# Cross network on one core: the last jobs in another order, with group 6's output transposes and store in other places of the queues

## The chip, the core and the metric

The kernel runs on one core of a Trainium2 chip. Matrix products run on TensorE (PE), evacuations of PSUM with the bias on ScalarE (ACT), products and sums in bf16 on VectorE (DVE); SyncE (SP) issues nearly all DMAs, GpSimd (POOL) has a few copies. The metric is the device time of one execution in microseconds (us).

## The reference

```python
B, F, D, L = 16384, 26, 16, 6          # Din = F * D = 416
x = x0                                 # (16384, 416) bf16
for l in range(L):                     # ws (6, 416, 416), bs (6, 416)
    x = x0 * (einsum('bd,de->be', x, ws[l]) + bs[l]) + x
return x
```

## The kernel before

**Groups, jobs, tiles.** The 16384 rows are cut into 8 groups of 2048 (g = 0 to 7). A job (g, l) is layer l of group g. The features lie on the partitions: 416 = 3 x 128 + 32. The three blocks of 128 output features are the job's three tiles (i = 0, 1, 2), each of four chunks of 512 rows (j); the last 32 features are the job's tail, and the tails of two or three jobs are computed together, in a "tail phase" (`tails`, L677). A chunk takes 13 slots of TensorE time in quarters: 12 for the three blocks of 128 input features and one for the 32. A tile's chunk goes PSUM -> ACT (adds the bias, writes `tw`) -> DVE (times x0, in pairs of chunks) -> DVE (plus x, writes the next layer's `x`).

**Order.** The list `order` (L322 to L328) says in which order the 48 jobs run; a job of layer l needs all tiles and the tail of layer l-1 of its group. `batches` cuts that list into tail phases. `items` (L943) is the list of tiles and phases. From tile 1 of job (0, 2) to tile 0 of job (7, 4) the items run as one stream (`stream`, L1005): each chunk is done as row-tiled matmuls of 32 input rows, and the string `ORDER` (L204) says, letter by letter, which chunk is given the next free row group; "|" is a tail phase. `replay` (L230) turns the string into a list with a place in time for each matmul (20 units are one matmul of 512 columns) and for each evacuation. What stands behind the stream runs as whole 128-row matmuls (`full`, L629) and 32-row ones (`rows32`, L657). In the last stream tile only the 32-row part is in the stream; its 12 full matmuls follow it.

**The end.** Job (7, 5) is not tiled like that: its output comes in natural layout (L1116 to L1232), in four rounds kk of four products, each of 128 rows x 416. A product goes through ACT (`nat_out`, L1180), then DVE multiplies it by x0 (`nat_mul`, L1185) and adds x (`nat_add`, L1191), and SP stores the round (`nat_store`, L1199). The x to be added must be in natural layout too: `rest_turn(t)` (L922) transposes tile t of x(7, 5) (which is what job (7, 4) wrote) by DMA into `x5n`, for t = 0 and 1; tile 2 and the tail are transposed by TensorE (`turn_last`, `turn_tails`) and copied by DVE (L1150) and ACT (L1163). `nat_add` of round 0 waits for all of these.

**Output of the other groups.** `output(g)` (L876) is called when the last tile and the tail of (g, 5) are both done. It issues on SP a DMA transpose for each tile (`turn(t)`, into the one buffer `ost`), one of the tail (into `ot3`), and the store; `spread` copies `ot3` into `ost`, on POOL for groups 0 to 5, on ACT for group 6. `ost` is one buffer, so group g+1's transposes wait for group g's store to land. `prefill` (L615) issues DMAs that rotate a tail by 32-partition steps, for a later job of the same group; `tails` calls it for each job of the phase, followed by `done_with`, which may call `output`. SP runs its queue in order: whatever waits there holds all that follows.

**The last items before the change**, in order: (5, 5), (7, 3) tile 0, a phase [(5, 5), (7, 3), (6, 4)], the rest of (7, 3), (6, 4), and (7, 4) tile 0, where the stream ends; then (6, 5) tiles 0 and 1, a phase [(7, 4), (6, 5)], (6, 5) tile 2, (7, 4) tiles 1 and 2, and job (7, 5).

Of the kernel before, what the change touches and what calls it, by code (L numbers as in the profile page):

```python
# [21 lines left out]
class Program:  # L22
# [176 lines left out]

SLOT = 20  # L200
FENCE, PHASE, CHANGE = 22, 52, 9
READ, NEXT, BACK, SECOND, PAIR, TAILS, SUMS = 19, 56, 70, 92, 56, 220, 240
LETTERS = "ABCDEFGHIJKLMNOPQRSTUVWXYZabcdefghijklmnopqrstuvwxyz0123456789"
ORDER = (  # L204
    "ABCDAJCXaFTMWDUNSLYBKTMZjGANDaMpCPUJCXIROEDBaTUJCITVCQLVCAXNaALVaQHNKUTBQKDRICbRK|AJDWQJDCfUNSDM"
    "dSbJECbURCTINWDUJSPAJCTAZSPUJCDVYOTJAaDYVKTENCbNUSDJAXSYJGPAVODNUDOJUTCIRCDUNSbAJTaMVKHQBCXQNCPI"
    "ZSDJQCDMVaTEJOXBUDOAZXOIRGDYBSXARLOYBXKMZG|QBPSIVDCPAZOXQJGDQBaTINCLAdSXJYOHRACTNUCPJUSDAVCXRMaL"
    "FUCXARWPYBKPAdaLUNCLMVTCNISDcBWPIRCLAVSbMBKPYVSHMB|CTMVCPIVCDUNaTIBaTVAKTNUGDMVSDINCXYJCDMVSbIFW"
    "PQBCTMVCPIVSDIBWTANKTYVODAZOTUJGDURODINCbUJODBMSbIVCTUBSPIVGDQVCTMJWDAZSXINGDUBSXIBKTAZKPcRGAZPW"
    "QBP|QBOLRECTBCUPZSAPRaXASJPUBKUDVSAPRKAbSNcDOUbFKDURKDIRCbQJOXBIODVAOTUJCLQVCDUNSbEJWDQVCTINCbUJ"  # L210
    "ODIBaTVAKTNUGDMVSDINCXBcXSNAKPAZWLAVKTYNGDYNSDYN|ICXJTACVQPCNAPeVAPeRYLWNQDKNbCIBWTYBSLMVCLMVCXM"
    "JSDAdWPQBLOQBbKNQCDdMWTZEODNUKTABOXAVCTcVOLERCDcRaPAJWbMRKHYBCXQNCPIZSDJQCDMVaDMJSbAJTOYVGDMVCjU"
    "N|ISDJTAKRMDJCQDNeITVGMbBWIDRWIDRKAbJSMDBObQJCDdOQXJaMDJWMTBKAXhSMDJOUDVKQPFCMDBaQfVKALRWMDJOUDV"
    "KATBOYjREWDROULBKUTBSIBLCUdCMLZSAbJSUDRKMXeFLQBCXMR|CPISFDQCTIBaDUZKDQJWbMBXOIZCLQBSbIdODIVCTUJO"
    "DIVODIBbCNYXKERDCUdTaIBTaJUOHAVCTMVKDUJSDAVCXQNKDYJWfAJWTMZGDMVCXcNS|IDJTECRCTANaDYVKTMFWDUBOXAN"
    "KXZQODZATOJUCLURODINCbIBWTJYOHAVCTMVKDUJSDIRDCUNSbBISbVAKPURCLMRWDINCXIBWTJgOHAVCTMVKDUJSDAVCXQN"
    "KDYJSfAJaPURGDMdCbUN|ISDJTECRCTANaDMVKTFYWDAVOTYJGXAVODNUDOJUTCIRODIBSbUJPCIVDQCZTMBaLMBaXIBWLQZ"
    "ODIZCXQZKPAJWDRMWDNUKTBISBDUORbAOZDaULNQGXJCQXBAWPRaIDRKUDJSUPGBAbVCMDVOYLFSUPBeMXRCM|RCPISFDQCT"
    "IBaTIVOHQBPCMVDOAZWPBUOLQBCfURODIdWPQZGDQNCbINWDINXGQBPAWBQPKVDIVSPAJODYJCXQKZPEBWDQNWLAVKTAJSAD"
    "OVYDNKTYBKbMVSHBeMXRCM|RCPISFDQCDMVaTIBSbUBTKMVCLMVSDIBSXIZDKURDSMJCbIBSXIZOHQBCTMVCPIVSDQJCTIBa"  # L220
    "DUZSLAJbQOVHAOBbUOBLUChTIVOALVOQDJCXQBiLMSVDKMBbWJMHCVASXdIDJSUPCJUDSVIDSBMbRCMLRCcbJOALVMaDJMaD"
    "JYOXRAO|ANXKQBLSABOXYRGLMVDWNACbNQWDNISDJAWfBcSXJMGbVQCPRCPISFDAeTUBKTMVCLUNSDMJTCIBWTIdOHQBPCMV"
    "DOAZWPBUKDQVCfIRWPYFCXQZCPIRWDJQWPEBCTAZSPUJCLAZCXMRaLUBWLAVLSgNXGIRCDUNS|IDJTAKRMDJCQbJWATVCQPJ"
    "WALBaUTBODUadTIGVATVOIDJWAXRKYPFCMDBaMTCZMLRWALRCAfROUDJeUTaBQPKVEDVSMDJOAfJCQXKZMDJWATJWMDVKMTB"
    "CARaXMBKPZUDWRIPaAJbCYVTO|EJDWQBPCNAbOVLQCJDUiRLaAJbSUNDKMXCBMTWJYHOAVPCMVDOUBPWIRDIORXENKLAUKBN"
    "CD"
)


def replay(tails, events, needs, keep, part):  # L230

# [14 lines left out]
    home, read, out, latest, due = {}, {}, [], [[]] * 4, list(events)  # L246

    def over(now):
        nonlocal act
# [8 lines left out]
    for letter in ORDER:  # L258
        if letter == "|":
            now, m = min(free), due.pop(0)  # L260
            parts = [(f - now) // SLOT for f in free]
            at = now + max((f - now) % SLOT for f in free)
            over(at)
            on = at + 3 * SLOT * m + PHASE
            moved = [on + SLOT * k for k in parts]
            for f in flight.values():
                f[1] = moved[f[2]] if f[1] == free[f[2]] else -9 * SLOT
            got = [banks.pop(0) for _ in range(m)]
            assert all(t <= at + 3 * SLOT * k for k, (t, _) in enumerate(got))
            for r in range(4):  # L270
                for k in range(parts[r]):
                    latest[r][-1 - k][0] = moved[r] - SLOT * (k + 1)
            for k, (_, b) in enumerate(got):
                if k == 1:
                    banks.append((on + SECOND, b))
                    continue
                start = max(act, on - CHANGE + READ)
# [28 lines left out]
def bass_standalone__cross_network_dcn__recsys_kernel(  # L306
# [7 lines left out]
    L = ws.shape[0]  # L314
# [223 lines left out]
    def evacuate_chunk(g, l, i, j, b, read):  # L538
# [33 lines left out]

        todo = [multiply, plus]
        if len(out_) == NJ:
            todo.append(lambda: finish_tile(g, l))
# [101 lines left out]
    def tails(batch, corners_last=False, banks=None):  # L677
# [38 lines left out]
        while later:  # L716
            load_group(later.pop(0))
# [158 lines left out]
    def output(g):  # L876

        s, s3 = xset[(g, L)], xtail[(g, L)]
        def turn(t, j0=0, j1=NJ):
            add("sp", lambda h: h.dma_start_transpose(  # L880
                ost[:, j0 * KK:j1 * KK, t * P:(t + 1) * P], xs[s][:, t * GC + j0 * CH:t * GC + j1 * CH]),
                reads=[("x", s, t, j) for j in range(j0, j1)], writes=[("ost", t, j) for j in range(j0, j1)],
                lane="ot" if g < LAST - 1 else f"ot_{t}{j0}", batch=g)

        turn(0)
        if g == LAST - 1:
            turn(1)
        add("sp", lambda h: h.dma_start_transpose(ot3[:, :, :], x3s[s3][:, :]),
            reads=[("x3", s3)], writes=["ot3"], lane="ot3", batch=g)
        if g < LAST - 1:  # L890
            spread("pool")
            turn(1)
            turn(2)
            store(g, 0, NJ)
        else:
            turn(2, 0, 2)
            turn(2, 2, NJ)
        free_x.append(s)
        free_3.append(s3)

# [30 lines left out]
                writes=[("x5n", j, t) for j in range(j0, j1)], lane=f"x5_{t}{j0}", batch=0)  # L931

    items = []
    where = {(b[0 if b in batches[4:-3] else min(1, len(b) - 1)], 0): b for b in batches[:-1]}
    where[((LAST - 1, L - 1), 1)] = batches[-1]
    behind = ("tile", (LAST, L - 2), 0)
    del where[((0, 0), 0)]
    where[((0, 1), 0)] = where.pop(((1, 0), 0))
# [4 lines left out]
        if (jb, i) in where:  # L943
            items.append(("tails", where[(jb, i)]))

    for i in range(1, NT):
        late = items.index(("tile", (LAST, L - 2), i))
        items.append(items.pop(late))


    single = 0
    k = 0
    while k < len(items):
        if items[k][0] == "tails":
            if single % 2 == 0:
                nxt = k + 1
# [3 lines left out]
                    k += 1  # L960
            single = 0
        else:
            single = 1 if items[k] == behind else single + 1
        k += 1

    W_LOAD = {(1, 0): 3, (0, 2): 4, (1, 1): 5}
# [12 lines left out]

    tiles_done = {}  # L980

    def finish_tile(g, l, n=1):
# [22 lines left out]
    def stream(run, keep, part):  # L1005
# [9 lines left out]
        place = {it: NJ * k for k, it in enumerate(tiles)}  # L1015
        needs = [[(t, place[(g, l - 1), t]) for t in range(NT if c < len(chunks) - keep else part)
                  if c - place.get(((g, l - 1), t), -99) < 30] for c, ((g, l), i, j) in enumerate(chunks)]
        plan, read, left = replay([quad(g, l, j)[0] for (g, l), i, j in chunks], [len(b) for n, b in due],
                                  needs, keep, part)
# [58 lines left out]
    for n, it in enumerate(items):  # L1078
# [200 lines left out]
```

## Time and profile before

| | |
|---|---|
| runs, median of 3 | 467.83 us (467.56 to 467.90) |
| profiled execution | 467.5 us, its span 465.7 us |
| PE, DVE, ACT busy | 99%, 87%, 81% of the span |
| granted TensorE clock | 0.997 |
| DMA | 53.77 MB, mean 115 GB/s |

The profile gives busy times of each engine, the groups of instructions by source line, the chain of waits that ended last, and a timeline. In a timeline row the first number is the start in us from the span's beginning, the second how long the row's instructions took together, "SPq" an instruction of SP's queue (a DMA being issued, not its transfer), and a note in brackets the idle time before it and who ended it.

### The profile page before, as it was taken

How to read it: one execution, taken by the hardware profiler on the slowest of the kernel's cores; microseconds unless marked ns; L12 is line 12 of the kernel's file. 1: busy time of each engine (PE TensorE's matmuls, PEld its weight loads, DVE VectorE, ACT ScalarE, POOL GpSimd, SP SyncE). 2: the span in 40 equal slices, each digit the busy share in tenths (PEclk: the TensorE clock that was granted, in tenths of full speed). 3: DMA queues.
4: the chain of work that ended last, by engine and by line, in shares of the span. 5: the costliest groups of instructions: out<-in, count | busy, mean ns of one | idle time of the engine just before them, and what ended most of it. 6: DMA issues, size and time to landing. Idle time of an engine off the chain costs nothing.

```text
span 465.7 us, 17469 instructions
## 1 busy us (share of the span) xinstructions
PE 458.9 (99%) x7827; PEld 263.8 (57%) x7833; DVE 404.2 (87%) x700; ACT 379.1 (81%) x608; POOL 6.8 (1%) x15
## 2 busy tenths in 40 slices
PE   9999999999999999999999999999999999999995
PEld 5444566555556677555655556565575566755442
DVE  2887998989989899979989898888989889898897
ACT  4687888788888888888878888788887887889785
POOL 1000000000000000000000000000000000000000
PEclk9999999999999999999999999999999999999998
DMA  8986949101002978084858437990100095027899
GB/s 229 185 177 144 160 113 190 29 3 26 1 4 38 158 210 155 22 141 149 149 92 154 145 78 141 160 296 23 25 2 4 25 148 172 14 49 169 183 161 292
DMA packets 139087, 53.77 MB, mean 115 GB/s; under 512 B 112762, under 2 KB 138500, under 8 KB 139012
## 3 DMA queue, kind: packets, MB, share of 16 engines
q1 hardware_dynamic: 138856, 52.54, 52.5%
q8 instruction: 61, 1.00, 0.9%
q10 hardware_dynamic: 156, 0.11, 0.1%
q14 instruction: 14, 0.11, 0.1%
HBM read 5.97 MB, written 13.63 MB: 42 GB/s over the span
## 4 chain that ended last, share of the span: by engine, by line
PE 93%; DVE 4%; DMA 1%; issue 1%; ACT 0%; SPq 0%; DVEq 0%
PE ps L1040 70%; PE ps L697 7%; PE ps L1044 6%; PE ps L650 6%; PE ps L638 2%; PE ps L685 1%; DMA wm<-in_ws_dram 1%; DVE x L1194 1%; DVE x L1188 1%; DVE x L528 1%; DVE tw L523 1%; PE ps L671 1%; ACT tw L514 0%; PE ps L789 0%; SPq L734 0%
## 5 line engine op out<-in xcount | busy, mean ns | idle before, releaser
L1040 PE MATMUL ps<-x,wm 32*128 32x512 bf16 x6000 | 356.0, 374 | 0.0
L550 ACT ACTIVATE tw<-ps,bias 128x512 bf16<-128x512 f32 x500 | 310.5, 688 | 46.4 <-PE ps L1040 35.9
L1040 PEld LDWEIGHTS ps<-x,wm 32*128 32x128 bf16 x6000 | 212.5, 92 | 127.7 <-ACT tw L550 4.1
L562 DVE TENSOR_TENSOR tw<-tw,x 128x1024 bf16<-128x1024 bf16 x250 | 168.2, 689 | 39.6 <-ACT tw L550 38.9
L567 DVE TENSOR_TENSOR x<-tw,x 128x1024 bf16<-128x1024 bf16 x250 | 163.5, 690 | 0.3
L1044 PE MATMUL ps<-x,w 32*128 32x512 bf16 x504 | 151.7, 374 | 0.0
L1044 PEld LDWEIGHTS ps<-x,w 32*128 32x128 bf16 x504 | 42.7, 92 | 6.6
L514 ACT ACTIVATE tw<-ps,bias 128x512 bf16<-128x512 f32 (+1 forms) x46 | 35.0, 839 | 12.0 <-PE ps L671 7.9
L650 PE MATMUL ps<-x,wm 128*128 128x512 bf16 x146 | 33.6, 379 | 1.0 <-issue 0.8
L697 PE MATMUL ps<-x,wm 128*32 128x512 bf16 x564 | 33.6, 380 | 0.0
L608 ACT ACTIVATE ts<-ps,bias 128x512 bf16<-128x512 f32 x33 | 21.0, 687 | 14.7 <-PE ps L685 14.7
L523 DVE TENSOR_TENSOR tw<-tw,x 128x1024 bf16<-128x1024 bf16 (+1 forms) x35 | 21.4, 627 | 4.9 <-ACT tw L514 4.7
L650 PEld LDWEIGHTS ps<-x,wm 128*128 128x128 bf16 x152 | 13.9, 98 | 19.0 <-issue 3.2
L697 PEld LDWEIGHTS ps<-x,wm 128*32 128x32 bf16 x564 | 13.5, 96 | 18.7 <-ACT tw L550 4.7
L528 DVE TENSOR_TENSOR x<-tw,x 128x1024 bf16<-128x1024 bf16 (+1 forms) x35 | 20.6, 624 | 0.0
L612 DVE TENSOR_TENSOR x<-ts,x 128x512 bf16<-128x512 bf16 x47 | 18.4, 420 | 0.4
L610 DVE TENSOR_TENSOR ts<-ts,x 128x512 bf16<-128x512 bf16 x33 | 13.0, 418 | 0.0
L604 DVE SCALAR_TENSOR_TENSOR ts<-ps,bias,x 128x512 bf16<-128x512 f32 x14 | 10.5, 748 | 2.2 <-PE ps L685 2.2
L909 POOL COPY ost<-ot 128x512 bf16<-128x512 bf16 x6 | 5.3, 890 | 411.3 <-DMA ot<-x 411.3
L1130 PE MATMUL ps<-wm,x 128*128 128x416 bf16 x48 | 9.8, 340 | 0.1
L1182 ACT ACTIVATE x<-ps 128x416 bf16<-128x416 f32 x16 | 7.6, 518 | 2.4 <-PE ps L1130 2.4
L799 DVE COPY x<-ps 128x512 bf16<-128x512 bf16 x5 | 2.0, 423 | 8.5 <-PE ps L789 8.5
(50 smaller groups left out, 76.9 us busy)
## 6 DMA issues: line engine op xcount, KB each, us to landing
out_dram<-ost SPq DMA_DIRECT2D x6, 1664.0 KB, 7.1
x<-x SPq DMA_DIRECT2D x24, 96.0 KB, 2.3
x<-in_x_dram SPq DMA_DIRECT2D x8, 208.0 KB, 4.4
x<-in_x_dram SPq DMA_DIRECT2D x4, 416.0 KB, 8.0
out_dram<-ost SPq DMA_DIRECT2D x2, 832.0 KB, 6.0
wm<-in_ws_dram SPq DMA_DIRECT2D x5, 312.0 KB, 3.4
x<-x SPq DMA_DIRECT2D x22, 64.0 KB, 2.0
out_dram<-x SPq DMA_DIRECT2D x3, 416.0 KB, 4.8
```

The costliest lines, as they stand in the source:

```text
L514: add("act", lambda h, a=a, w=w, b0=b0: h.activation(tw[r][:, a * CH:(a + w) * CH], psum[:, b0 * CH:(b0 + w) * CH], ACT_F.Identity, bias=b ...
L523: add("dve", lambda h, a=a, e=e: h.tensor_tensor(tw[r][:, a * CH:e * CH], tw[r][:, a * CH:e * CH], x0s[s0][:, i * GC + a * CH:i * GC + e * ...
L528: add("dve", lambda h, a=a, e=e: h.tensor_tensor(xs[so][:, i * GC + a * CH:i * GC + e * CH], tw[r][:, a * CH:e * CH], src(i, a, e), ALU.ad ...
L550: add("act", lambda h: h.activation(tw[r][:, j * CH:(j + 1) * CH], bank(b), ACT_F.Identity, bias=bias[:, i, l:l + 1], scale=1.0), reads=[( ...
L562: add("dve", lambda h: h.tensor_tensor(tw[r][:, o], tw[r][:, o], x0s[s0][:, c], ALU.mult), reads=[("tw", r, k) for k in both] + [x0_tok(s0 ...
L567: add("dve", lambda h: h.tensor_tensor(xs[so][:, c], tw[r][:, o], src(i, a, a + 2), ALU.add), reads=[("tw", r, k) for k in both] + [stok(i ...
L608: add("act", lambda h: h.activation(ts[r][:, :], bank(b), ACT_F.Identity, bias=bias[:, 3, l:l + 1], scale=1.0), reads=[("ps", b), "bias"], ...
L612: add("dve", lambda h: h.tensor_tensor(x3s[so][:, :], ts[r][:, :], res, ALU.add), reads=[("ts", r)] + rtok, writes=[("x3", so), ("x3", so, ...
L650: add("pe", lambda h, t=t, j=j, k=k, w=w: h.matmul(bank(banks[j])[:, k * w:(k + 1) * w], wm[l][:, t, ecols], src(t, j, j + 1)[:, k * w:(k ...
L697: add("pe", lambda h, t=t, j=j, src=src, l=l, b=b, ro=ro, qo=qo: h.matmul(psum[qo, b * CH:(b + 1) * CH], wm[l][:, t, NT * P:D], src(t, j, ...
L1040: add("pe", lambda h, l=l, t=t, j=j, b=b, q=q, ecols=ecols, src=src, kw=kw: h.matmul(bank(b), wm[l][q, t, ecols], src(t, j, j + 1)[q, :], ...
L1044: add("pe", lambda h, l=l, b=b, q=q, ecols=ecols, s3=s3, kw=kw: h.matmul(bank(b), w3[l][q, ecols], s3[q, :], **kw), reads=tok3 + [("w3", l ...
```

## The change

`order`'s last jobs become (6, 3), (5, 5), (7, 2), (6, 4), (7, 3), (6, 5), (7, 4), (7, 5). The last three phases are written out: [(5, 4), (6, 3), (7, 2)], [(5, 5), (6, 4), (7, 3)], [(6, 5), (7, 4)]. The two late tiles of (7, 4) are no longer moved behind (6, 5) by hand. So the stream, which ends at (7, 4) tile 0 as before, now holds the three tiles of (6, 5) and the phase [(6, 5), (7, 4)] as well; behind it only (7, 4) tiles 1 and 2 are left. Within the stream a phase is no longer put behind the tile that follows it when the count of tiles is odd, so most phases stand one tile sooner; `ORDER` is a new string, and `replay` has a new condition: a chunk of (g, l) starts no sooner than 600 units after the phase of (g, l-1) ended (`ROTATE`).

In the queues: the tile transposes of groups 5 and 6 are issued by `finish_tile` as each tile ends, those of groups 0 to 4 by `output` as before. In `tails`, all jobs' `prefill` rotations are issued ahead of `done_with`, and group 6's tail transpose right behind its phase. Group 6's `spread` (ACT) and its two stores (SP) are issued behind the last tile of (7, 4).

The sequence on SP from the phase of (5, 5) on is, before: group 5's tail transpose, its tiles 1 and 2, its store, four rotations, `rest_turn(0)`, group 6's tiles 0 and 1, its tail, its tile 2 in two halves, `rest_turn(1)` in two halves, group 6's two stores, and the stores of group 7. After: four rotations, group 5's tail transpose, its store, group 6's tile 0, its tail, its tile 1, its tile 2 in two halves, `rest_turn(0)`, `rest_turn(1)` in two halves, and the stores.

```diff
-    order[-6:] = [(5, 5), (7, 3), (6, 4), (7, 4), (6, 5), (7, 5)]
+    order[-8:] = [(6, 3), (5, 5), (7, 2), (6, 4), (7, 3), (6, 5), (7, 4), (7, 5)]
...
+    batches[-3:] = [[(5, 4), (6, 3), (7, 2)], [(5, 5), (6, 4), (7, 3)], [(6, 5), (7, 4)]]
...
+            if after[c] is not None:
+                start = max(start, past[after[c]] + ROTATE)
...
+        for g, l in batch if corners_last else ():
+            prefill(g, l + 1)
+            filled.add((g, l + 1))
+        if (LAST - 1, L - 1) in batch:
+            turn_tail(LAST - 1)
         for g, l in batch:
-            if corners_last:
-                prefill(g, l + 1)
-                filled.add((g, l + 1))
             done_with(g, l)
...
+    def output(g):
+
+        s, s3 = xset[(g, L)], xtail[(g, L)]
+        if g < LAST - 2:
+            turn(g, 0)
         if g < LAST - 1:
+            turn_tail(g)
             spread("pool")
-            turn(1)
-            turn(2)
+            if g < LAST - 2:
+                turn(g, 1)
+                turn(g, 2)
             store(g, 0, NJ)
-        else:
-            turn(2, 0, 2)
-            turn(2, 2, NJ)
...
-    for i in range(1, NT):
-        late = items.index(("tile", (LAST, L - 2), i))
-        items.append(items.pop(late))
...
-    while k < len(items):
+    while items[k] != ("tile", (0, 2), 1):
...
+    def finish_tile(g, l, n=1, i=None):
+        if l == L - 1 and g > LAST - 3:
+            turn(g, i)
...
         if (g, l) == (LAST, L - 2) and i < NT - 1:
-            if i:
-                spread("act")
             rest_turn(i)
+        elif (g, l) == (LAST, L - 2):
+            spread("act")
+            store(LAST - 1, 0, 2)
+            store(LAST - 1, 2, NJ)
...
-    store(LAST - 1, 0, 2)
-    store(LAST - 1, 2, NJ)
```

More of the change, by code (lines that the diff above doesn't have):

```diff
@@ L201 @@
 FENCE, PHASE, CHANGE = 22, 52, 9
-READ, NEXT, BACK, SECOND, PAIR, TAILS, SUMS = 19, 56, 70, 92, 56, 220, 240
+READ, NEXT, BACK, SECOND, PAIR, TAILS, SUMS, ROTATE = 19, 56, 70, 92, 56, 220, 240, 600
 LETTERS = "ABCDEFGHIJKLMNOPQRSTUVWXYZabcdefghijklmnopqrstuvwxyz0123456789"
 ORDER = (
[L205 to L226, printed above, removed]
@@ new lines @@
+    "ABCDAJCXaFTMWDUNSLYBKTMZjGANDaMpCPUJCXIROEDBaTUJCITVCQLVCAXNaALVaQHNKUTBQKDRICbRK|AJDWQJDKbQBSDQ"
+    "dKbMFCbMVSDMJCXIZSDJAXSIBKTYBSLUZDKMVTCMJSDIZOTEBPCUBPSAZLCRUKDdQaXJAWTYJGPAVODNUDOJUTCIBCbUNKDI"
+    "daTMVCPJUaTFA|RODMLFCAXYSBPQCZPIWRALROUDKBQXaJATKVASLVMCLBYSXNICDZMWDVMSDNICfVISbBSbJUOHAVCTMVKD"
+    "UJSDIRPCANbCVMSLYBLORUHBeMXRCM|RCPISFDAWTIBKDUZKDgRKbMVCXJMaTFAODVATOJUCLURODARCfYRWLARXOANLYBaL"
+    "QVCLcNSXEKRDAWNDUOJTAKRATCNDUaNLcGBTMWZHSBMbCVM|RCPISFDQCDMVaTIBSbUBTKMVCLMVSDANSXAdTOJUDJCYTVAO"
@@ new lines @@
+    "BPcWJDUeRbIGVPCUBTMWBPIWRDICTVCMJDWcRLaMXFCMTBaIDVSIPFCUPRCADRaUPFKQDaNQXCIBXSIZHOQBPCMVLCAZDaRM"
+    "DaNIXCVcTOJYXSFA|RODMLFCAXYSBPQCZPIWRALROUDKBQXaJATKVASLVMGDBYSXJATCZMSLVEODNUCDRAafJQPGBbMCZULS"
+    "BIeTZODIVCTUJODIVODIBbCNYXCIVSPAdaLUBWLMRHKBYXRCM|RCPISFDQCDMVaTEJOXBUPCAZPSUBPKQVDKQBTaAZKDQZKX"
+    "MFSDYBXOAdKXQNCLMZSDINTCANWDVgSLENXKBUTCAVPYCVLMSBDMeVLSYFXCMVTCMJDWIZPSFAPCUBPSIVHCURPCMBaDMZLC"
+    "IVTaMFDOYVDMJWfAVK|MBXKNALWNQCDNQCbJAWTBQePJCfQZWPERCPAWJPgSHARCTYNKDUJSDIRPCANbSBYSLVATKUNCLMVS"
@@ L227, with replay @@
+    "UPCJAbSVIDSJUDRKUPBKAbRWMDJCYTVOIHBAaXBQOLVcGDVQODJMeXRAK|MBXKNALWNQCDNAWbJAWTBSPcJUGbNQKHVEOLBC"
+    "DANCXMKBLYCVTYeNHAaVfQGJ|ADCRUbCJTAgSJbMiVLQWBTMVCD"
 )
-def replay(tails, events, needs, keep, part):
+def replay(tails, events, needs, after, keep, part):
     n = len(tails)
@@ L245, in replay @@
     banks = [(0, 0), (0, 1), (0, 2), (0, 3), (84, 4), (84, 5), (178, 6), (178, 7)]
-    home, read, out, latest, due = {}, {}, [], [[]] * 4, list(events)
+    home, read, out, latest, due, past = {}, {}, [], [[]] * 4, list(events), []
     def over(now):
@@ L874, in load_last, with turn @@
                 reads=["brow"], writes=[("brow", j)], lane="brow", batch=0)
[L876 to L880, printed above, removed]
+    def turn(g, t):
+        s = xset[(g, L)]
+        halves = ((0, 2), (2, NJ)) if (g, t) == (LAST - 1, NT - 1) else ((0, NJ),)
+        for j0, j1 in halves:
+            add("sp", lambda h, j0=j0, j1=j1: h.dma_start_transpose(
                 ost[:, j0 * KK:j1 * KK, t * P:(t + 1) * P], xs[s][:, t * GC + j0 * CH:t * GC + j1 * CH]),
@@ L933, in bass_standalone__cross_network_dcn__recsys_kernel @@
     items = []
-    where = {(b[0 if b in batches[4:-3] else min(1, len(b) - 1)], 0): b for b in batches[:-1]}
-    where[((LAST - 1, L - 1), 1)] = batches[-1]
+    where = {(b[0 if b in batches[4:-3] else min(1, len(b) - 1)], 0): b for b in batches[:-3]}
+    where.update({((5, 4), 1): batches[-3], ((6, 4), 1): batches[-2], ((6, 5), 1): batches[-1]})
     behind = ("tile", (LAST, L - 2), 0)
@@ L962, in bass_standalone__cross_network_dcn__recsys_kernel @@
         else:
-            single = 1 if items[k] == behind else single + 1
+            single += 1
         k += 1
@@ L1017, in stream @@
                   if c - place.get(((g, l - 1), t), -99) < 30] for c, ((g, l), i, j) in enumerate(chunks)]
+        phase = {jb: k for k, (n, b) in enumerate(due) for jb in b}
         plan, read, left = replay([quad(g, l, j)[0] for (g, l), i, j in chunks], [len(b) for n, b in due],
-                                  needs, keep, part)
+                                  needs, [phase.get((g, l - 1)) for (g, l), i, j in chunks], keep, part)
         at = list(ring)
```

19 lines of the change are left out of this document (14 added, 5 removed).

## The prediction, as it stood before the run

> **What bounds the kernel now.** First the page: where the time is, and the chain that ended last.
>
> ```profile
> span 465.7 us, 17469 instructions
> PE 458.9 (99%) x7827; PEld 263.8 (57%) x7833; DVE 404.2 (87%) x700; ACT 379.1 (81%) x608; POOL 6.8 (1%) x15
> PE 93%; DVE 4%; DMA 1%; issue 1%; ACT 0%; SPq 0%; DVEq 0%
> ```
>
> TensorE carries 93% of the chain; the stream has no gap to win. The rest is DVE, and the chain in order of time shows where: PE to 442.8 us, then without a break DVE to 462.4. So the end is asked for next: the timeline of DVE and ACT.
>
> ```profile
> 446.88 1.36 DVE L523 TENSOR_TENSOR tw<-tw,x 128x1024 bf16<-128x1024 bf16 x2
> 452.04 1.38 DVE L1150 COPY x<-ps 128x1024 bf16<-128x1024 bf16 x2
> 453.34 1.14 DVE L1188 TENSOR_TENSOR x<-x,x 128x832 bf16<-128x832 bf16 x2
> 454.39 1.08 DVE L1194 TENSOR_TENSOR x<-x,x 128x832 bf16<-128x832 bf16 x2
> ...
> 442.76 4.75 ACT L514 ACTIVATE tw<-ps,bias 128x1024 bf16<-128x1024 f32 x7 [0.98 <-PE ps L671]
> 447.54 0.63 ACT L907 ACTIVATE ost<-ot 128x512 bf16<-128x512 bf16 x1
> 448.07 2.41 ACT L514 ACTIVATE tw<-ps,bias 128x512 bf16<-128x512 f32 x4
> ```
>
> No DVE row has a bracket: from 446.88 on it has no wait worth naming. L1194 at 454.39 is the first `nat_add`, which needs `rest_turn`'s transposes. ACT is late for the last tile because of a backlog and the `spread` copy (L907). Third, SP's timeline, for what each queued DMA waits behind:
>
> ```profile
> 427.55 0.41 SPq L916 DMA_DIRECT2D out_dram<-ost  x1
> 428.00 1.96 SPq L444 DMA_DIRECT2D x<-x  x1
> ...
> 435.23 1.81 SPq L928 DMA_TRANSPOSE x<-x  x1
> 438.85 5.67 SPq L880 DMA_TRANSPOSE ost<-x  x2
> 444.57 1.69 SPq L888 DMA_TRANSPOSE ot<-x  x1
> 446.39 2.62 SPq L880 DMA_TRANSPOSE ost<-x  x2
> 449.05 2.72 SPq L928 DMA_TRANSPOSE x<-x  x2
> 451.95 1.87 SPq L916 DMA_DIRECT2D out_dram<-ost  x2
> ```
>
> SP issues from 442.6 to 453.2 with hardly a pause; `rest_turn(1)` (L928, two halves at 449.05 and 450.4) stands behind all of group 6. Last, the load of the DMA engines by stretches (columns from the end: GB/s, DMA share, clock):
>
> ```profile
> 442.58:452.00 9.42, 9.21 (x67) 4.26 (x61) 8.94 (x20) 8.29 (x14) 0.00 (x0) 1.00 0.88 170
> 456.00:464.00 8.00, 4.73 (x32) 2.15 (x30) 6.25 (x14) 4.14 (x8) 0.00 (x0) 0.95 1.11 333
> ```
>
> The engines are nearly full on both sides: on transposes at 170 GB/s, then on stores at 333. After 446.88 the end is set by DVE, with the DMA queue close behind.
>
> **The stream and TensorE.** Work is only moved. The stream gains three tiles and a phase of two tails. Two phases starting at 238.26 and 266.08 lie 2574 of `replay`'s units apart: 27.82 us, so one slot of 20 units is 0.216 us. Three tiles are 3 x 13 x 0.216 = 8.4 us; the phase is 24 of the 36 column matmuls that take 2.06 us, 1.4, with corners and the change of shape 1.9; the new string leaves 0.1 us less empty: 10.2 us later. The twelve full matmuls of (7, 4) tile 0, loaded from 429.44, move to 439.6. Behind them stand two tiles: 2.70 (429.44 to 432.14) + 0.33 (32-row part, 445.57 to 445.90) + 2.70 + 0.33 + 2.60 (445.90 to 448.50) = 8.66, so job (7, 5) starts at 448.26 instead of 448.50: **-0.24**. The phases that stand one tile sooner, and ROTATE, cost the order no slot; group 4's load falls behind a rotation that waits for the phase at 79.8, near 86 instead of 68.7, and is used at 176.
>
> **ACT and DVE at the end.** The stream's last evacuation starts near 441.3 (its place in the order), then four of about 0.6 for tile 0, to 444.3; tile 1's banks are full at 444.8 to 445.4, so ACT is through it at 447.25 and through tile 2 at 449.6 (before: 450.48), since `spread` now stands behind. DVE is the slower one: from 438.9 on it has (6, 5) tiles 1 and 2, (7, 4) tiles 0 and 1, 16 operations of 0.61 (1.29 for two, overlapped) = 9.8, one wait for ACT of 0.3, then eight of 0.335 (2.7), to 451.7 instead of 452.12. The copies and the products of (7, 5) also wait for TensorE, which gains 0.24, so no more than that is counted: the first `nat_add` could start at 454.2 instead of 454.39, its second half at 454.7 instead of 454.90: **-0.2**. Moving `spread` earns nothing more, as DVE covers it; ACT has a pause of 0.9 ahead of `nat_out`, where it fits.
>
> **SP.** Group 6's first transpose needs its tile on DVE and group 5's store landed. The phase of (5, 5) moves to 419.5; rotations at 423.3 and, behind five more DVE operations, 425.2 (0.6 us per DMA), group 5's tail transpose 426.4, landing 2.95 later, POOL copy 0.93, store 430.5, landing 6.8 later (the row of 427.55), 437.3. DVE reaches (6, 5) tile 0 only at 438.2, because its second pair stands behind the tail of (7, 4). So the series starts at 438.2, 0.6 sooner than the 438.85 of before, but `rest_turn(0)` (435.23 before) is now inside it: tile 0 of (7, 4) ends at 446.4 instead of 435.2. The work in the series grows from four tile transposes and a tail to five and a tail. Issue by rows: first 2.0 (1.8 to 2.9), tail 1.7 (1.3 to 2.1), tile 1 2.3 (1.9 to 2.9), tile 2 in halves 2.7, `rest_turn(0)` 2.8 (1.8 to 2.9: third and fourth transposes in a row take 2.2 to 3.0 each), gaps 0.2: 11.7. `rest_turn(1)` starts at 449.9 and 451.3, where before it was 449.05 and 450.4; group 6's store at 452.7 instead of 451.95. Bounds: all rows shortest, 448.5 (DVE's data), all longest, 452.2.
>
> A half landed 4.7 and the next 4.1 after its issue: 454.6 and 455.4 to 455.9. DVE wants them at 454.2 and 454.7. What was 0.4 to 0.6 us of cover becomes a wait of 0.7 to 1.2 for the second half, and DVE's queue behind it has no gap up to 462.4, so it goes to the end in full: -0.2 + 0.9 = **+0.7**. With the shortest rows it is -0.2; with all the longest at once, and 4.7 to land, +2.5 by the first half and +3.4 by the second. The stores of 832 KB and 416 KB behind move alike.
>
> [...]
>
> **The sum.** 467.5 + 0.7 = 468.2 for an execution like the profiled one, which lay 0.33 under the median: 468.5.
>
> **Rivals.**
> - A, the queue is no limit. A tile of 128 x 2048 bf16 is 0.52 MB; at the stores' 333 GB/s it takes 1.6 us, under SP's own 1.9 to 2.0 per issue, and the series is 2.0 + 1.7 + 2.0 + 2.6 + 2.0 + 0.2 = 10.5. `rest_turn(1)` then starts at 448.8 and all is there in time: -0.2, 467.6. For it: the tile transposes of 420.41 took 2.2 each. Against: those at 375.42 took 2.9.
> - B, slower: group 5's store lands late. Only where it lands after 438.2 does it count, and then every us is one at the end. That store landed 8.9 after its issue in the execution's other case of that size (383.32), and the rotations took 5.4 us at 428.00 instead of the 2.6 I give them: 2.1 to 4.9 later, less the 0.9 of cover, on top of the +0.7 but eased by a queue that is then empty: near 470.0.
> - C, faster: the end is set by the DMA queue, and group 6's store leaves earlier. Its last tile is on DVE at 443.9 instead of 446.97, its tail transpose goes at 440.2 instead of 444.57. If SP comes to the store before 451 (ACT's copy is done at 450.25), the 1.66 MB leave up to 1.6 us sooner, the last store lands in 2.0 (the row of 64 KB transfers) instead of 2.8, and with DVE's -0.2: -1.0, 466.8. Against: SP has one more transpose ahead of the store.
> - That the change doesn't do what it says: the tiles and the tail of group 6 do end sooner, the store does not by my sum; this is part of the forecast.
>
> **How the numbers follow.** The likeliest: forecast 0.45, own range 467.9 to 469.5; A 0.22 (467.2 to 467.9); B 0.17 (469.4 to 471); C 0.16 (466.4 to 467.1). 0.2% is 0.94 us, about what a measurement of this kernel can tell from no change: 466.9 to 468.8. Faster: 0.14 of C and 0.03 of A = 0.17. Slower: all of B and 0.20 of the forecast = 0.37. Same: 0.46. The range 467.0 to 470.2 leaves out most of C and the upper part of B, 0.2 together.
>
> **What would show it.** In the changed profile: (7, 5)'s first matmul near 448.3; `spread` behind ACT's last tile near 449.6; SP's first transpose of group 6 at 438.2, waiting for DVE (if for a DMA, B); the time from there to `rest_turn(1)` (11.7 against 10.5 for A); a wait of DVE ahead of `nat_add` round 0, for a DMA; the last DVE operation at 462.9 to 463.2. Wrong at once if the last phases do not stand near 419.5 and 433.3: the stream would then have stalls that its order does not show.

## The result, and the profile after

The changed kernel takes 468.46 us (median of 20 runs, 467.91 to 469.53), the kernel before 467.89 on the same chip (20 runs, 467.30 to 468.32): ratio 1.0015 [1.0009, 1.0022]. It is slower, by 0.57 us, less than the 0.94 us (0.2%) that the prediction counts as no change. A second series on the same chip as the first experiments gave 1.0021 [1.0013, 1.0030]. The forecast was 468.5.

The profiled execution of the changed kernel took 469.46 us, 1.0 above its own median; before's lay 0.3 under its own. So a profile of the changed kernel run once more, `after_again` (467.94 us, 0.5 under its median), is read beside it: the two together bracket the usual run. First the page of the profiled execution after.

```profile
span 467.7 us, 17583 instructions
PE 458.6 (98%) x7888; PEld 266.7 (57%) x7893; DVE 403.9 (86%) x700; ACT 379.4 (81%) x609; POOL 8.8 (2%) x15
PE 90%; SPq 3%; DVE 3%; DMA 2%; issue 1%; ACT 1%; DVEq 0%; ACTq 0%
```

TensorE's busy time is what it was (458.6 against 458.9): nothing was won or lost in the stream. DMA has 2% of the chain, before 1%. The timeline of DVE shows where it stands at the end.

```profile
452.04 1.38 DVE L1163 COPY x<-ps 128x1024 bf16<-128x1024 bf16 x2
453.33 1.14 DVE L1201 TENSOR_TENSOR x<-x,x 128x832 bf16<-128x832 bf16 x2
455.56 0.59 DVE L1207 TENSOR_TENSOR x<-x,x 128x832 bf16<-128x832 bf16 x1 [1.08 <-DMA x<-x]
456.85 0.59 DVE L1207 TENSOR_TENSOR x<-x,x 128x832 bf16<-128x832 bf16 x1 [0.70 <-DMA x<-x]
...
463.63 0.65 DVE L1207 TENSOR_TENSOR x<-x,x 128x416 bf16<-128x416 bf16 x2
```

Copy and `nat_mul` (L1201) stand to 0.01 us where they stood before. Ahead of both halves of `nat_add` (L1207) there is now a bracket: DVE waits 1.08 and 0.70 for the transposes of `rest_turn(1)`. The timeline of SP after says why they are late.

```profile
427.00 1.81 SPq L896 DMA_TRANSPOSE ot<-x  x1
431.40 0.41 SPq L929 DMA_DIRECT2D out_dram<-ost  x1
439.70 3.07 SPq L888 DMA_TRANSPOSE ost<-x  x1
442.83 1.25 SPq L896 DMA_TRANSPOSE ot<-x  x1
444.13 5.18 SPq L888 DMA_TRANSPOSE ost<-x  x3
449.42 5.41 SPq L941 DMA_TRANSPOSE x<-x  x3
455.00 1.14 SPq L929 DMA_DIRECT2D out_dram<-ost  x2
```

Group 6's first transpose starts at 439.70, though its tile was done on DVE at 438.61: it waited for group 5's store (issued 431.40) to land. All that follows is one unbroken row of issues, `rest_turn(0)` and both halves of `rest_turn(1)` in the row of 449.42, and group 6's store only at 455.00 (before: 451.95). In the timeline of `after_again`, SP and then DVE, the same row starts with the data:

```profile
430.51 0.41 SPq L929 DMA_DIRECT2D out_dram<-ost  x1
438.36 1.91 SPq L888 DMA_TRANSPOSE ost<-x  x1
...
447.83 5.14 SPq L941 DMA_TRANSPOSE x<-x  x3
453.15 1.13 SPq L929 DMA_DIRECT2D out_dram<-ost  x2
```

```profile
455.07 0.59 DVE L1207 TENSOR_TENSOR x<-x,x 128x832 bf16<-128x832 bf16 x1 [0.38 <-DMA x<-x]
```

DVE waits 0.38, and the store goes at 453.15. So there are two ways in which the changed kernel runs, by whether group 5's store has landed by 438.4; six further profiles, of variants with that store unsplit, show both (starts at 438.4 and 438.6 in two, 439.2 to 439.6 in four). That would fit the wider spread of its spans (465.9 to 467.7 in 20 executions; 465.5 to 466.3 in 25 of the kernel before). The spread of its times has a second part, outside the span: in 3 of the 20 executions the time is 2.6 to 2.7 over the span, in the other 17, and in all 83 of the kernel before that have a span on record, 1.75 to 2.03. What that part is isn't shown.

Last, the DMA engines at the end. In this view each digit is the busy share of 0.2 us, from 460.0 on; first before, then after.

```profile
DMA  9999999999999999999970000000000000000000
GB/s 329 333 333 333 329 333 333 333 333 333 333 329 329 337 333 324 341 329 324 329 208 21 21 0 0 0 0 0 0 0 0 0 0 0 0 0 0 0 0 0
```

```profile
DMA  9999999999999999999999999999999200000000
GB/s 324 345 337 333 329 325 329 345 329 329 337 325 329 333 337 324 333 349 304 341 337 329 320 349 329 316 341 320 350 312 325 71 21 0 0 0 0 0 0 0
```

The engines are full to 464.1 before and to 466.2 after, 2.1 later; the span is 2.0 longer. They have no gap in either, so in neither does the last store leave an idle queue: it stands behind a backlog of output. In `after_again` they are full to 464.5, and its span of 466.0 is 0.3 longer than before's.

The stretch ahead of that differs. First before, each digit 0.125 us from 451.0 on; then two rows after (last columns: DMA share, GB/s).

```profile
DMA  9999797999999000000049999999999999999999
GB/s 209 213 205 168 152 234 168 201 219 203 109 70 20 0 2 10 10 8 10 10 88 283 291 291 373 346 406 353 399 346 393 326 286 300 353 379 353 346 353 333
```

```profile
454.00:456.00 2.00, 2.00 (x18) 0.84 (x17) 0.92 (x2) 1.75 (x4) 0.00 (x0) 1.00 1.05 192
456.00:458.00 2.00, 2.00 (x16) 0.95 (x17) 1.26 (x4) 1.48 (x3) 0.00 (x0) 1.00 1.08 341
```

Before, the engines stand nearly empty from 452.5 to 453.5, although group 6's store is on SP from 451.95: its first half takes SP 1.24 us, against 0.63 at most after, and the output flows only from 453.6. What held it isn't shown. After, transposes fill the engines until 456.0, and from there the output flows without a gap (330 to 341 GB/s in each 2 us up to 466). So the issue of the store moved by 3.05 us, the start of the flow by 2.4 and the end by 2.1. The experiments ask which of the two delays, DVE's wait or the backlog, makes the time.

### The profile page after: what moved, and what is told of

Same layout as the page of the kernel before. It is cut to its first block, busy times and chain, and to the rows that moved or that the text cites. A ratio compares the mean times of both kernels' runs of the same rounds, so it can differ in the third digit from the quotient of the medians.

```text
span 467.7 us, 17583 instructions
## 1 busy us (share of the span) xinstructions
PE 458.6 (98%) x7888; PEld 266.7 (57%) x7893; DVE 403.9 (86%) x700; ACT 379.4 (81%) x609; POOL 8.8 (2%) x15
## 4 chain that ended last, share of the span: by engine, by line
PE 90%; SPq 3%; DVE 3%; DMA 2%; issue 1%; ACT 1%; DVEq 0%; ACTq 0%
PE ps L1051 71%; PE ps L702 7%; PE ps L1055 6%; PE ps L655 4%; SPq L412 2%; PE ps L690 1%; DMA x<-in_x_dram 1%; DVE x L1207 1%; PE ps L643 1%; SPq L741 1%; DVE x L1201 1%; DMA x<-x 1%; ACT tw L519 1%; DVE x L533 1%; DVE tw L528 0%
## 5 line engine op out<-in xcount | busy, mean ns | idle before, releaser
L1051 PE MATMUL ps<-x,wm 32*128 32x512 bf16 x6144 | 364.4, 374 | 0.0
L555 ACT ACTIVATE tw<-ps,bias 128x512 bf16<-128x512 f32 x512 | 318.7, 688 | 49.6 <-PE ps L1051 36.5
L1051 PEld LDWEIGHTS ps<-x,wm 32*128 32x128 bf16 x6144 | 219.5, 92 | 129.1 <-ACT tw L555 3.8
L567 DVE TENSOR_TENSOR tw<-tw,x 128x1024 bf16<-128x1024 bf16 x256 | 171.9, 687 | 42.6 <-ACT tw L555 41.3
L572 DVE TENSOR_TENSOR x<-tw,x 128x1024 bf16<-128x1024 bf16 x256 | 167.1, 690 | 0.2
L1055 PE MATMUL ps<-x,w 32*128 32x512 bf16 x516 | 154.6, 374 | 0.0
L519 ACT ACTIVATE tw<-ps,bias 128x512 bf16<-128x512 f32 (+1 forms) x36 | 27.9, 861 | 9.3 <-PE ps L676 7.4
L655 PE MATMUL ps<-x,wm 128*128 128x512 bf16 x123 | 28.4, 379 | 1.0 <-issue 0.6
L655 PEld LDWEIGHTS ps<-x,wm 128*128 128x128 bf16 x128 | 11.7, 98 | 15.7 <-issue 2.8
L528 DVE TENSOR_TENSOR tw<-tw,x 128x1024 bf16<-128x1024 bf16 (+1 forms) x29 | 17.3, 613 | 2.9 <-ACT tw L519 2.8
L533 DVE TENSOR_TENSOR x<-tw,x 128x1024 bf16<-128x1024 bf16 (+1 forms) x29 | 16.7, 609 | 0.0
```

Of the source, the lines that this page charges most:

```text
L519: add("act", lambda h, a=a, w=w, b0=b0: h.activation(tw[r][:, a * CH:(a + w) * CH], psum[:, b0 * CH:(b0 + w) * CH], ACT_F.Identity, bias=b ...
L528: add("dve", lambda h, a=a, e=e: h.tensor_tensor(tw[r][:, a * CH:e * CH], tw[r][:, a * CH:e * CH], x0s[s0][:, i * GC + a * CH:i * GC + e * ...
L533: add("dve", lambda h, a=a, e=e: h.tensor_tensor(xs[so][:, i * GC + a * CH:i * GC + e * CH], tw[r][:, a * CH:e * CH], src(i, a, e), ALU.ad ...
L555: add("act", lambda h: h.activation(tw[r][:, j * CH:(j + 1) * CH], bank(b), ACT_F.Identity, bias=bias[:, i, l:l + 1], scale=1.0), reads=[( ...
L567: add("dve", lambda h: h.tensor_tensor(tw[r][:, o], tw[r][:, o], x0s[s0][:, c], ALU.mult), reads=[("tw", r, k) for k in both] + [x0_tok(s0 ...
L572: add("dve", lambda h: h.tensor_tensor(xs[so][:, c], tw[r][:, o], src(i, a, a + 2), ALU.add), reads=[("tw", r, k) for k in both] + [stok(i ...
```

## The experiments

Three theories. **Q**: the late series on SP is longer by one tile's transpose, `rest_turn(1)` lands late, DVE waits, and this wait is the loss. **R**: only group 5's store, landing late, holds the series. **S**: the end is set by the sum of late DMA work; DVE's wait only goes with it. Kernels named "before" start from the kernel before, the others from the changed one. All times below are medians; ratios are to the kernel before, run on the same chip in the same rounds.

**`after_again`**, the changed kernel as it is.

> The changed kernel once more, as the measure for the others beside it: about 0.6 us over the kernel before. In its profile: SP's first transpose of group 6 waits for the landing of group 5's store, and the first nat_add has waits of DVE for a DMA, 0.5 to 1.8 us together. If the waits of DVE vary from execution to execution with the landing of that store (6.8 to 8.2 us after its issue), the spread of the times over the rounds is that of the store.

468.47 us (11 runs, 467.94 to 470.47), before 467.63: 1.0021 [1.0013, 1.0030]. The loss repeats.

**`store5_sooner`**: group 5's tail transpose ahead of the second pair of rotations, so that its store leaves sooner.

```diff
+            if (g, l) == (LAST, L - 3) and (LAST - 2, L - 1) in batch:
+                turn_tail(LAST - 2)
...
-            turn_tail(g)
+            if g < LAST - 2:
+                turn_tail(g)
```

> Group 5's tail transpose is issued ahead of the second pair of rotations instead of behind it, so that its store goes some 1 to 2 us sooner (near 429.5 to 430.5 instead of 431.4). Theory Q (the longer series of transposes delays rest_turn, and it begins when both group 5's store has landed and DVE has done the tile): the series begins 1.0 sooner, at 438.6 with DVE, and the end comes 0.5 to 1.0 sooner than in the changed kernel where that one waits for the store; some wait of DVE ahead of nat_add stays, so the time is 0 to 0.3 over the kernel before. Theory R (all of the loss is the landing of the store): no wait is left and the time is 0.2 under the kernel before. Theory S (the end is set by the sum of the DMA work): also 1.0 sooner, as the work begins sooner.

468.52 (12 runs): 1.0020 [1.0009, 1.0031], no gain. In its profile the store left at 430.22 and the series started at 438.64, with DVE's tile, and yet DVE waited 0.15 and 0.72 in `nat_add`. With the store in time the loss is there: R falls as the cause, though it remains what makes some executions worse. Q and S missed too: both expected it sooner than the changed kernel, by 0.5 to 1.0 where that one waits for the store.

**`rest_ahead`**: the two half transposes of group 6's tile 2 behind `rest_turn(1)`, nothing else.

```diff
-        if l == L - 1 and g > LAST - 3:
+        if l == L - 1 and g > LAST - 3 and (g, i) != (LAST - 1, NT - 1):
...
+            turn(LAST - 1, NT - 1)
```

> The two half transposes of group 6's tile 2 are issued behind rest_turn(1) instead of ahead of it; the sum of the DMA work is the same. Theory Q: rest_turn(1) starts 2.7 us sooner, DVE has no wait ahead of nat_add, and its last operation comes near 462.4 as in the kernel before; the store of group 6 is issued near 456.5 and the end is set by DVE or by the store behind it: 0.5 to 1.8 sooner than the changed kernel. Theory S: the waits of DVE go as well, but the last stores land no sooner than in the changed kernel, and the time is the same within 0.3.

469.54 (5 runs, 469.08 to 469.96): 1.0041 [1.0029, 1.0053], 1.1 us over the changed kernel. Both theories missed, and the profile says more than any other run. SP, then DVE, then the DMA engines from 460.0:

```profile
439.62 2.87 SPq L888 DMA_TRANSPOSE ost<-x  x1
...
455.23 1.43 SPq L929 DMA_DIRECT2D out_dram<-ost  x2
```

```profile
454.30 1.09 DVE L1208 TENSOR_TENSOR x<-x,x 128x832 bf16<-128x832 bf16 x2
...
461.65 0.65 DVE L1208 TENSOR_TENSOR x<-x,x 128x416 bf16<-128x416 bf16 x2
```

```profile
DMA  9999999999999999999999999999999200000000
GB/s 345 341 345 279 354 366 350 349 345 333 300 354 350 341 345 341 341 333 325 341 349 316 324 345 321 333 337 329 333 329 329 67 17 0 0 0 0 0 0 0
```

DVE no longer waits: its last operation ends at 462.30, 1.98 sooner than in the profile after. And the span is the same, 467.7, to the tenth. The two executions have the series' start in common (439.62 and 439.70), the store's issue (455.23 and 455.00) and the end of the full engines (466.2). So without any wait of DVE the stores end as late as with 1.78 us of it. The edit doesn't take away the wait alone: the store of group 6 now has to wait for its own last tile to land (it is issued 0.79 behind the end of the transposes' row), and between 454 and 458 the engines moved 234 GB/s against 267 in the profile after. S left that out, and missed by it. That the wait cost nothing in the profile after itself is read from the engines there: from 456.0 to 466.2 they had no gap, so no store of group 7 came too late for them. Q is refuted in its last step, from wait to end.

**`no_rest0`**: `rest_turn(0)` left out, so that what is added for tile 0 is not x(7, 5) but what the buffer held before.

```diff
-        if t == 0:
+        if t == 1:
             add("pool", lambda h: h.memset(warm[:, :], 0.0), writes=x0_all(s5) + x03_toks(s5) + ["x5 free"])
...
-            rest_turn(i)
+            if i:
+                rest_turn(i)
```

> rest_turn(0) is left out (tile 0 of the x to be added in job (7, 5) is not brought into natural layout), so that the series has four tile transposes and a tail, as in the kernel before. Theory Q: rest_turn(1) starts 2.7 us sooner, no wait of DVE is left, and the time is 0.2 to 0.5 under the kernel before, 0.8 to 1.8 under the changed kernel. Theory R: the wait for the store is still there, so rest_turn(1) is late by the 1.1 us that the store costs, and the time is over the kernel before. Theory S: 2 to 2.8 us under the changed kernel, by the DMA time of one transpose.

466.55 (7 runs, 466.04 to 467.79): 0.9977 [0.9966, 0.9987], 1.92 under the changed kernel, between Q's 0.8 to 1.8 and S's 2 to 2.8. R, which expected a loss, is out: the series started at 439.46, behind the late store. Group 6's store left at 451.83 in its profile, DVE had no wait, and the engines ran dry between the stores (from 460.0):

```profile
DMA  9948999998996499800000000000000000000000
GB/s 329 337 125 279 345 358 349 354 304 292 354 354 212 150 333 320 271 21 0 0 0 0 0 0 0 0 0 0 0 0 0 0 0 0 0 0 0 0 0 0
```

The digits below 9 between full ones are stores that wait for DVE (SP waits for `nat_add` four times, 6.7 us in all). Here DVE ends last: span 464.6, 2.5 after DVE's last operation (before 3.3, after 3.4, `rest_ahead` 5.4). One tile's transpose in the late series is what the change costs, and all else in it together would be worth about 1.1 us (467.63 less 466.55), an upper bound, since the transfer is gone here and not moved.

**`before_rest0_late`**: the opposite; in the kernel before, `rest_turn(0)` moved from 435 to just ahead of `rest_turn(1)`, nothing else.

```diff
-            rest_turn(i)
+                rest_turn(0)
+                rest_turn(1)
```

> The kernel before, with rest_turn(0) taken from its early place on SP (435.2) and issued just ahead of rest_turn(1), behind group 6's tile 2: the one trait of the changed kernel's queue, without its order of jobs. Theory Q (a fifth tile transpose in the late series) and theory S (the late DMA work sets the end): rest_turn(1) starts 2 to 2.8 us later (451.1 to 451.9), DVE has waits of 1.0 to 2.0 ahead of nat_add, the time is 1.0 to 2.2 over the kernel before. If the order of the jobs is what costs, it is the same as the kernel before within 0.3.

469.79 (5 runs, 469.33 to 470.23), before 467.85: 1.0041 [1.0028, 1.0055], +1.94. SP, then DVE:

```profile
449.38 6.22 SPq L928 DMA_TRANSPOSE x<-x  x3
455.77 1.13 SPq L916 DMA_DIRECT2D out_dram<-ost  x2
```

```profile
456.46 0.59 DVE L1195 TENSOR_TENSOR x<-x,x 128x832 bf16<-128x832 bf16 x1 [1.66 <-DMA x<-x]
457.63 0.59 DVE L1195 TENSOR_TENSOR x<-x,x 128x832 bf16<-128x832 bf16 x1 [0.57 <-DMA x<-x]
```

The rows of the changed kernel appear in the old one: the waits, and the store 3.8 later than 451.95. The engines are full to 467.0. From both sides, then, the one tile's transfer costs 1.9 us where it stands late. The profiled execution is the slowest of the five, and its engines also stood nearly empty from 453.9 to 455.2, so not all of its 2.9 us at the end of the full engines are the tile's bytes.

**`split_store5`**: group 5's store in two: the 384 features of its tiles as soon as tile 2 is transposed (410.14 in the profile), the last 32 at the old place (430.84).

```diff
-            store(g, 0, NJ)
+                store(g, 0, NJ)
+            elif g == LAST - 2:
+                store_part(g, NT, NT + 1, "outb")
...
+            if (g, i) == (LAST - 2, NT - 1):
+                store_part(g, 0, NT, "out")
```

> The changed kernel with group 5's store in two: the 384 features of the three tiles as soon as these are transposed (near 408), the 32 of the tail by a store of their own behind the POOL copy. Nothing then holds group 6's first transpose but DVE (438.2 to 438.6). Theory Q with the store as the cause of the spread from run to run: the times lie closer together than the changed kernel's 467.9 to 470.5, with the median 0.2 to 0.6 under its 468.5, still over the kernel before by 0.2 to 0.6, because the fifth transpose stays in the series.

467.86 (11 runs, 467.50 to 469.16), before 467.85: 1.0007 [0.9998, 1.0016]. The series started at 438.14 with the data. By the ratios that is 0.4 to 0.7 us better than the changed kernel, with intervals that just overlap; what it takes away would be the executions in which group 5's store lands late. The times do not lie closer together, as was expected (1.66 us from lowest to highest, 1.62 in the changed kernel), but the spans do (465.7 to 466.7): the highest time, 469.16, has a span of 466.2.

**`tail_pe_before`** and **`tail_pe_after`**: group 6's tail transposed by TensorE, with two ACT copies, in place of the DMA and `spread`, in either kernel.

```diff
+    def tail_out(b):
...
+        for kk in range(KK):
+            add("pe", lambda h, kk=kk: h.transpose(
+                psum_t(b)[:, kk * P:(kk + 1) * P], x3s[s][:, kk * P:(kk + 1) * P], ident[:, :]),
...
+        for j in (0, 2):
+            add("act", lambda h, j=j: h.activation(dst[:, j:j + 2], sp_[:, j:j + 2], ACT_F.Copy),
...
+    tail_out(b3)
+    store(LAST - 1, 0, 2)
+    store(LAST - 1, 2, NJ)
```

> The kernel before with group 6's tail transposed by TensorE (four transposes of 128x128 and two copies by ACT of 0.33 in place of the DMA transpose and of ACT's copy of 0.63), so that the late series of DMAs is one short transpose (1.7 us on SP) less. In the kernel before, DVE ended 3.3 us before the span and in the run without rest_turn(0) 2.5 us. Theory S (DMA work left over at the end also counts): 0.3 to 0.8 under the kernel before. Theory Q alone (only a wait of DVE for rest_turn counts, and there is none here): the same within 0.2.

> The same in the changed kernel: rest_turn(1) starts 1.3 to 1.7 us sooner, DVE's waits ahead of nat_add go or fall under 0.4. Theory Q: 0.6 to 1.2 under the changed kernel, 467.3 to 467.9 here. Theory S: the same or more, down to 467.0. If the store of group 5 is all (R): no change from the changed kernel.

In the kernel before 467.90 (1.0000 [0.9992, 1.0009]), in the changed one 469.02 (9 runs, 468.04 to 469.92; 1.0026 [1.0016, 1.0036]): no gain. The first is what Q expected; S expected 0.3 to 0.8. In the profile of the first the stores have gaps (the engines fall to 42 GB/s between 460 and 461), so there DVE, which was close behind, sets the end. In the second Q and S both expected a gain, of 0.6 to 1.2 or more, and missed. In the changed kernel's profile the wait of DVE is gone, but the store leaves at 452.77, only 0.38 sooner than in `after_again`, and the engines are full to 464.05, 0.4 sooner. Then, from 460.0:

```profile
DMA  9999999999999999999921100000000000000000
GB/s 325 329 333 394 312 304 320 316 308 329 320 333 337 329 337 333 320 345 321 325 75 42 29 21 21 21 17 21 12 0 0 0 0 0 0 0 0 0 0 0
```

21 GB/s is a sixteenth of 333, as if one of the 16 engines ran on alone, for some 1.3 us (about 0.5 before, 0.3 after), and the span ends behind it: at 466.8 instead of the 465.6 that the other executions' distance of 1.4 to 1.6 would give. Such a tail is longest, 0.8 to 1.3 us, in three of the four kernels that transpose a piece by TensorE, and 0.6 at most in the others; what ties the two isn't shown. This run doesn't tell whether the wait or the backlog is the loss.

**`spread_back`**: the ACT `spread` copy at its old place, ahead of the last tile.

```diff
+            if i:
+                spread("act")
...
-            spread("act")
```

> The changed kernel with ACT's spread copy (0.63 us) back in its old place, ahead of the evacuation of the last tile of (7, 4). ACT is then 0.6 later with that tile, DVE, which comes to it only at 449.2 to 449.4, is not: the forecast's claim that moving the copy earns nothing says the same as the changed kernel within 0.2. If ACT's chain counts, 0.4 to 0.6 over it.

468.34 (11 runs), before 467.74: 1.0016 [1.0007, 1.0025]. As the changed kernel: where that copy stands is worth nothing that these runs can tell.

**`rest0_copy`**: `rest_turn(0)` as a plain copy of the same 512 KB, in pieces of 256 bytes, at the same place; tile 0 of x(7, 5) arrives untransposed.

```diff
-            add("sp", lambda h, j0=j0, j1=j1: h.dma_start_transpose(
+            add("sp", lambda h, j0=j0, j1=j1: (h.dma_start if t == 0 else h.dma_start_transpose)(
...
```

> The changed kernel with rest_turn(0) as a plain DMA copy of the same 0.52 MB between the same buffers, not transposed (the values added for tile 0 of job (7, 5) are then not the right ones). [...] By the trace (167 to 200 GB/s in transposes, 333 in stores): the copy takes 1.6 us of the DMA engines, the series is 1.0 to 1.3 shorter and the time 0.6 to 1.3 under the changed kernel's, near the kernel before or 0.5 under it.

468.66 (11 runs): 1.0023 [1.0014, 1.0031], no better than the transpose (1.0021 in `after_again`), where 0.6 to 1.3 us less was expected. SP:

```profile
448.90 0.70 SPq L941 DMA_DIRECT2D x<-x  x1
449.65 4.43 SPq L941 DMA_TRANSPOSE x<-x  x2
454.26 1.14 SPq L929 DMA_DIRECT2D out_dram<-ost  x2
```

The copy takes SP 0.70 instead of 2 to 3, but the half transpose behind it, 1.34 in the row of the kernel before at 450.43, is held until 452.40: what SP saves it waits for right behind. The price is that of the transfer through the engines, not of SP's issuing, and a copy in pieces of 256 bytes pays it as a transpose does.

**`half_pe_split`** and **`half_pe_before`**: the second half of group 6's tile 2 by TensorE and one ACT copy (1.08 us) in place of a DMA transpose; the first with `split_store5`, the second in the kernel before with `spread` late.

```diff
+    def half_out(b):
...
+        for a in (2, 3):
+            for kk in range(KK):
...
+        add("act", lambda h: h.activation(dst, psum_t(b).rearrange("p (a f) -> p a f", f=P), ACT_F.Copy),
```

> The changed kernel with group 5's store in two (as in split_store5) and the second half of group 6's tile 2 transposed by TensorE, in the wait ahead of job (7, 5)'s first products, and copied by ACT (1.0 us, in its pause ahead of nat_out). One half of a tile less in the late DMA series: by the measured 1.9 to 2.0 us for a whole tile, 0.9 to 1.0 under split_store5, so 0.3 to 0.9 under the kernel before. If TensorE's eight transposes or ACT's copy are not covered, 0.5 of that is lost.

> The same half tile by TensorE in the kernel before, with the spread copy behind the last tile, so that ACT frees the bank in time. There no DVE wait for rest_turn is left to remove; the DMA left over at the end is 1.4 us less: by the run without rest_turn(0), where the last store landed 2.1 us after its issue instead of 2.8, 0.3 to 0.8 under the kernel before. tail_pe_before, which took out a smaller transpose, came out the same: if that holds here too, the end of the kernel before is DVE's alone and this is the same within 0.2.

`half_pe_split` 467.38 (11 runs, 467.12 to 468.28), before 467.74: 0.9996 [0.9988, 1.0005]. `half_pe_before` 467.60: 1.0002 [0.9993, 1.0011]. In the first, SP comes to the store as early as in `no_rest0`:

```profile
446.56 5.06 SPq L951 DMA_TRANSPOSE x<-x  x3
451.80 1.13 SPq L939 DMA_DIRECT2D out_dram<-ost  x2
```

It is the best complete version, 0.5 under `split_store5` by the ratios, but can't be told from the kernel before, where 0.3 to 0.9 under it was expected. `half_pe_before` is the same as the kernel before, the second of its two readings: its store is issued no sooner (452.04 against 451.95), and its engines stand nearly empty from 452.5 to 453.8, so the half tile less only widens that gap.

**All executions side by side** (us; from each kernel's profile):

| kernel | DVE waits in `nat_add` | DVE's last operation ends | engines full until | span |
|---|---|---|---|---|
| before | 0 | 462.4 | 464.1 | 465.7 |
| after_again | 0.38 | 462.5 | 464.5 | 466.0 |
| half_pe_before | 0 | 463.0 | 464.4 | 466.0 |
| split_store5 | 0.91 | 462.9 | 464.9 | 466.4 |
| store5_sooner | 0.87 | 463.4 | 465.3 | 466.8 |
| spread_back | 1.47 | 463.5 | 465.4 | 466.9 |
| rest0_copy | 1.40 | 463.6 | 465.5 | 466.9 |
| after | 1.78 | 464.3 | 466.2 | 467.7 |
| rest_ahead | 0 | 462.3 | 466.2 | 467.7 |
| before_rest0_late | 2.23 | 465.1 | 467.0 | 468.4 |
| tail_pe_after | 0 | 462.3 | 464.05, one to 465.7 | 466.8 |

In the first ten the span ends 1.4 to 1.6 us after the engines stop being full; after DVE's last operation it is 3.0 to 5.4. That range comes from `rest_ahead` alone (the other nine have 3.0 to 3.5), so the distances by themselves don't tell the two apart: DVE is never far behind the queue. The engines tell them apart. The backlog is 3.41 MB of output (832 KB x 2, 416 KB x 3, and the last 416 KB in parts), 10.2 us at 333 GB/s, and in every execution of the table but `before_rest0_late`, in which stores and transposes mix, the engines are full for 10.0 to 10.5 us from where the output begins to flow to their end. They never ran dry in between, so DVE kept no store from them. The three left out (`no_rest0`, `half_pe_split`, `tail_pe_before`) have gaps in the stores, and in them DVE leads. So in the kernel before and in the changed one alike, what ends last is this backlog. It stands behind the transposes ahead of it and group 6's store (in the profile after the transposes fill the engines until 456.0, and the output flows from there).

## Why the prediction was right, point by point

The time was right (468.46 for 468.5), and so was the mechanism up to its last step. Predicted, then the profile after, then `after_again`:

| step | predicted | after | after_again |
|---|---|---|---|
| group 5's store issued | 430.5 | 431.40 | 430.51 |
| series of transposes starts | 438.2, on DVE | 439.70, on the store | 438.36, on DVE |
| from there to `rest_turn(1)` | 11.7 | 12.4 | 11.5 |
| (7, 5)'s first matmul | 448.26 | 448.50 | 448.22 |
| first `nat_mul` | 0.2 sooner | 0.0 | 0.29 sooner |
| DVE waits in `nat_add` | 0.7 to 1.2 | 1.78 | 0.38 |
| group 6's store issued | 452.7 | 455.00 | 453.15 |
| DVE's last operation ends | 462.9 to 463.2 | 464.28 | 462.51 |

**The stream.** The last phases stand at 419.80 and 433.63 (419.5 and 433.3 forecast): the count of slots held. The -0.24 came in one execution and not in the other.

**The series.** 11.7 from rows was near both values (11.5 and 12.4), and rival A's 10.5 came in neither. That what counts in the row is the queue and not SP's own time was right: in `rest0_copy` the copy took SP 0.70 us, and the half transpose behind it 2.71 instead of 1.34.

**From the wait to the end: the failed step.** The text said that DVE sets the end "with the DMA queue close behind" and that the wait "goes to the end in full". The wait came (1.78 and 0.38), but in the profile after the engines move output without a gap from 456.0 to 466.2, and `rest_ahead` has no wait and the same end. The order is the other way round: the DMA queue sets the end with DVE close behind. The sign that I had and misread was the row of 333 GB/s at a share of 1.11 to 464.0: the queue was full while the last stores were issued, and it was the bound. The two rows shown also leave out 452 to 456, where the engines stood nearly empty for a microsecond.

**The number was in part luck.** Both delays come from the same late transposes, so both move the end the same way, but the sum priced the wrong one. By the queue, the forecast's own store at 452.7 would have cost little: the output flows about 1.0 us behind the issue in the profiles after and `after_again`, so from 453.7 or 453.8, against 453.6 before; that is 0.1 to 0.2 us (an estimate from these rows) where the sum has 0.7. The store left later than forecast, at 453.15 and 455.00, and that made up the difference. A slip beside it: the longest rows named for the series add up to 451.9, not 452.2; neither the sum nor the range rests on it.

**Rivals.** A fell with `rest0_copy` and the 11.5 to 12.4. In the stretch from 449 to 453 the engines move 200 GB/s at a share of 1.08 in the profile after, and 197 at 0.88 in `rest0_copy`, where a plain copy in small pieces stands in for the transpose. So my reading of the 170 GB/s, that transposes are slow and stores are not, was too narrow: a plain copy in pieces of 256 bytes went no faster there. B came true in part, in part of the executions: 1.1 us late in the profiled one, not 2.1 to 4.9, and `store5_sooner` shows the loss without it. C had the right bound and the wrong direction: the queue does set the end, and the store leaves later, not sooner. Its own "against" (one more transpose ahead of the store) was the answer.

## What to carry to other kernels

Look at the DMA engines in the last stretch before calling a compute engine the bound: if they are full up to the end, as here to 464.1 before and 466.2 after, the time is that at which the last big stores begin to flow plus their backlog (10.0 to 10.5 us here), and a wait that the chain shows ahead of an add may be worth nothing (1.78 us in the profile after, none in `rest_ahead`, and the same span of 467.7). A transfer moved from an idle stretch of the queue into the row that leads to the last stores was paid for there (1.9 us for 512 KB, found by adding it to the one kernel and taking it from the other). To tell a wait from a backlog that moves with it, look for a gap in the engines between the first of the late stores and the end, and change the order so that the wait goes.

## What the runs showed of the hardware

A plain copy on chip of 512 KB in 256-byte pieces landed 4.6 us after its issue, no sooner than the transposes ahead and behind (medians 4.1 and 4.4), at 197 GB/s with the engines 0.88 full, while the stores move at 333 GB/s (456 to 464 before). The copy's issue returned early (0.70 us), and the next transpose was held: 2.71 us on SP, against 1.34 in the kernel before. After the stores the DMA engines run on at 21 GB/s, a sixteenth of 333, for between 0.2 and 1.3 us before the span ends; that this is one of the 16 engines alone is a reading of the number. What makes it long stays open, as does why the first half of group 6's store took SP 1.24 us before with the engines nearly empty, and why group 5's store, issued 0.4 to 0.9 later, takes 1.2 to 1.3 longer to land (7.8 to 7.9 us of waiting for it against 6.6).
